# The tail of V with two halves side by side, and three reorderings, in a fused retention, expert-attention and mixing kernel

## The chip, the cores and the metric

The kernel runs on one core of a Trainium2 chip. The metric is the device time of one execution in microseconds; where several executions are timed, the median stands for them. All products are made in float32 by splitting each operand into a high part and a low part (xh and xl for x, WH and WL for the projection weights): a product is the sum of high times high, high times low and low times high, three matmuls into one PSUM accumulator.

## The reference

Eight batches, 576 positions, 8 retention heads of 64, then 4 experts with heads of 64, model width 512. Cut to what matters:

```python
# 1. retention: decayed causal linear attention
Dmat = np.where(rel >= 0, gamma[:, None, None] ** rel[None, :, :], 0.0)
x = ((q @ k.T / 8) * Dmat) @ v                 # per batch and head -> [B, S, 512]
# 2. top-2 of 4 experts, each a causal softmax attention with its own Q, K, V, Wo
logits = x @ w_gate                            # softmax over the top two -> w
a = softmax(causal(scale * (x @ wq[e]) @ (x @ wk[e]).T))
out += mask * w * (a @ (x @ wv[e]) @ wo[e])
# 3. mixing over positions and channels
theta = x @ w_theta
y = w_tok_r @ (x * cos(theta)) + w_tok_i @ (x * sin(theta))
u = x + y
return u + relu(u @ w_ch)
```

## The kernel before

The 576 positions are cut into five chunks, four of 128 rows and a tail of 64 (`ROWS`, lines 22 to 25). The kernel has three stages on the same core. In the first, retention of one batch and the attention of the batch before it run interleaved; the second makes theta and the cosines of the finished outputs; the third does the mixing. All the edits lie in the first stage.

**The loop of attention (lines 644 to 729).** A unit is one batch b, one pair p of experts and one chunk m of queries; there are 80 (`nu`), ten to a batch. At step t TensorE gets, in this order: the scores of unit t (`at_scores`, matmuls at L336), projections named by `more` in `SLOTS` (L45), the transposes of the probabilities of unit t-1 (`at_trans`, L383, with the copy PSUM to PT at L388), then what `between` names: "O" for outputs of a finished group of chunks (`at_out`, L402), or one of the visits R1 to R5. The groups of chunks are (0), (1, 2) and (3, 4). `ready` is the list of output groups finished by an earlier step, `outs` that of this one. The last batch has no next one to work for; its ten steps, and one more, follow `LAST` (L57) instead: projections, the product of theta's weights with Wo (`F0`, `F1`), and early tiles of the second stage (`T`); there all finished outputs run at the end of their own step.

**A visit (`ret_step`, L203).** It advances the retention of batch b+1 by one chunk c: `scale` (L124) has GpSimd multiply the chunk's values by the decay into vp; `ret_state` (L151, matmuls at L158) adds to the 64x64 states S; `ret_scores` (L135, matmuls at L143) makes the scores, masked into sm by VectorE (L147); `ret_values` (L164, matmuls at L173 and L180) makes the outputs px, which VectorE scales into xt (L190), ScalarE copies to xh (L192) and GpSimd subtracts into xl (L193); then `ret_values` issues the loads of a later chunk through `loads` (L113). These products are pairs of 64x64 blocks on two quadrants of TensorE, two generators side by side: the values as `off`, states and scores as `diag`. If the visit has outputs to do (`mid`), it runs all but the last four steps of the values, then the outputs, then one more state beside the last four steps. Of the visits of a batch, R1 and R2 have both outputs in their middle and such a state after; the visit R4 has outputs, but no state after. The first batch has no attention beside it: `ret_first` (L219) and lines 538 to 568 run its chunks one after the other at the start, where the decay product of a later chunk is issued behind the xl of the chunk at hand (L197).

**Projections.** `proj_v` (L262) makes V and the gate's logits of one chunk: its rows of x are the stationary operand, 4 blocks of 128 channels, 260 columns of weights moving (256 of V, 4 of the gate), three products: twelve matmuls for a chunk, the tail included, whose stationary operand has 64 columns. ScalarE copies PSUM to V and to the logits (L277, L278). `proj_qk` (L235, L246) makes U from Q and KN from K; KN goes through four DMA transfers on SP's queue into KK (L252), the layout that the scores read.

**The order of the work.** TensorE's order in the first stage is the order of the code (`manual_schedule`, L412). The other engines and SP's queue of DMA issues are put in order by a planner before the run, which places each instruction by its priority and its simulated readiness; `issue_after` in the code holds an instruction behind another in that order. SP issues one transfer after the other, each on the waits that it needs, so a transfer that waits holds those behind it. PSUM has eight buffers named w that all of the first stage share. The tiles of the retention live in the pool `ret`; it is released at step nu-11, and the pools for Wo, theta's weights and the outputs (w2, wol, wa) take its space. At that step `fuse_load` (L507) issues eight loads of 256 columns of Wo (`wost`) and four of theta's weights (`th`), and `load_o` (L573) loads the outputs (`ol`) and the gate's rows (`og`) of a finished batch, which GpSimd multiplies (L580). At step nu-10 `fuse_split` (L527) splits all eight `wost` tiles into high and low parts, on ScalarE (L106) and VectorE (L107). Meanwhile the float64 weights of the third stage are converted in small jobs (`convert`, L461), eight small instructions on VectorE, ScalarE and GpSimd each.

Of the kernel before, what the change touches and what calls it, by code (L numbers as in the profile page):

```python
# [10 lines left out]
F32 = mybir.dt.float32  # L11
# [12 lines left out]
NCH = 5  # L24
# [39 lines left out]
def tile_kernel(ctx: ExitStack, tc: tile.TileContext, qk, kv, w1, wo, wot, wd, cst, out):  # L64
# [43 lines left out]


    MARK = {}  # L110
    QKT, KVT, XT, VP, SM, RAW = {}, {}, {}, {}, {}, []

    def loads(b, c):  # L113
        R = ROWS[c]
# [46 lines left out]
        o = SB[(k + 1) % 4]  # L161
        MARK["S"] = nc.vector.tensor_add(o, pS, SB[k % 4]) if k else nc.scalar.activation(o, pS, AF.Copy)

    def ret_values(b, c, first=False):  # L164

        R = ROWS[c]
        t, vp = QKT[b, c], VP[b, c]
        px = ps1.tile([128, 4, R], F32, name="w", bufs=WB, padded_shape=[128, 4, 128])
        for j in range(R // 64):
            sm = SM.pop((b, 2 * c + j))  # L170
            for x in range(4):
                for s in range(2):
                    nc.tensor.matmul(px[half(1 - s), x, half(j)], vp[half(s), j, x, :], sm[half(s), x, :],  # L173
                                     start=j == 0 and x == 0, stop=False, skip_group_check=True)
                yield
        for j in range(R // 64):
            k = 2 * c + j
            for x in range(4 if k else 0):
                for s in range(2):
                    nc.tensor.matmul(px[half(1 - s), x, half(j)], SB[k % 4][half(s), x, :], t[half(s), x, half(j)],  # L180
                                     start=False, stop=False, skip_group_check=True)
                yield
        for x in (QKT, KVT, VP):
            x.pop((b, c))
        cs = slice(c * C, c * C + R)
        if c == 0:
            XT[b] = (w1p.tile([128, 4, S], F32R, name="xh", bufs=1),
                     w1p.tile([128, 4, S], F32R, name="xl", bufs=1))
        xt = ret.tile([128, 4, R], F32, name="xt", bufs=2, padded_shape=[128, 4, 128])
        MARK["xt"] = nc.vector.tensor_mul(xt, px, gt[:, :, cs])  # L190
        xh, xl = XT[b]
        MARK["xh"] = nc.scalar.activation(xh[:, :, cs], xt, AF.Copy)  # L192
        MARK["xl"] = nc.gpsimd.tensor_sub(xl[:, :, cs], xt, xh[:, :, cs])  # L193
        nx = (b, c + LDB) if c + LDB < NCH else (b + 1, c + LDB - NCH)
        if nx[0] < B:
            loads(*nx)
        if RAW and first and c:  # L197
            with tc.issue_after(MARK["xl"].ins):
                scale()

    BLOCKS = {0: ((0, (4,)),), 1: ((0, (5, 6)),), 2: ((0, (7, 8)),), 3: ((1, (0, 1)), (1, (2,))), 4: ((1, (3,)),)}

    def ret_step(b, c, mid=None):  # L203

        if RAW:
            scale()
        diag = [ret_state(b, 2 * c + 1)] if c < NCH - 1 else []
        diag += [ret_scores(b + x, ks) for x, ks in BLOCKS[c] if b + x < B]
        last = (b, c + 1) if c < NCH - 2 else (b + 1, 0) if c == NCH - 1 and b + 1 < B else None
        off = ret_values(b, c)  # L210
        n = (12, 16, 16, 16, 8)[c]
        for _ in zip_longest(chain(*diag), islice(off, n - 4) if last and (mid or c == NCH - 1) else off):
            pass
        if mid:
            mid()
        for _ in zip_longest(ret_state(last[0], 2 * last[1]) if last else (), off):
            pass

    def ret_first(b, c, nx, scores):  # L219

        diag, off = [], []
        if 0 <= c < NCH - 1:
            diag.append(ret_state(b, 2 * c + 1))
        diag += [ret_scores(nx[0], ks) for ks in scores]
        if nx and nx[1] < NCH - 1:
            diag.append(ret_state(nx[0], 2 * nx[1]))
        if c >= 0:
            off.append(ret_values(b, c, True))
        for _ in zip_longest(chain(*diag), chain(*off)):
            pass  # L230

# [30 lines left out]
    def proj_v(b, c):  # L262
# [6 lines left out]
        R = ROWS[c]  # L269
        cs = slice(c * C, c * C + R)  # L270
        ps = ps1.tile([128, NV], F32, name="w", bufs=WB, padded_shape=[128, 512])
        for x, W in ((xh, WH), (xh, WL), (xl, WH)):
            for kt in range(4):
                nc.tensor.matmul(ps[:R], x[:, kt, cs], W[:, kt, w0:w0 + NV], start=x is xh and W is WH and kt == 0,  # L274
                                 stop=x is xl and kt == 3)
# [248 lines left out]
            nc.sync.dma_start(th.bitcast(F32), TT[kt])  # L524
            FW[kt] = (th, FW[kt])

    def fuse_split():  # L527
        for a in FP:
            with tc.issue_after(MARK["act"].ins), tc.issue_after(MARK["dve"].ins):
                split(*a)  # L530

# [28 lines left out]
    for k in range(4):  # L560
        with tc.issue_after(MARK["xt"].ins), tc.issue_after(MARK["xh"].ins):
            split_w1(0, k)
    w1s.release()
    work(-1, "v1")
    ret_first(0, 3, (0, 4), [(8,)])
    work(-1, "v2 k00")
# [86 lines left out]
    for t in range(nu + 1):  # L653
# [27 lines left out]
        if b < B - 1:  # L681
            if between[:1] == "R":
                c = int(between[1])
                x = b + 1
                def mid():
                    for o in ready:
                        at_out(*o)
# [3 lines left out]
                outs = ready + outs  # L691
        else:
            work(b, between)
            for o in ready + outs:
                at_out(*o)
            outs = []
        work(b, after)


# [7 lines left out]
        if t == nu - 11:  # L707
            assert not jobs[0]
            ret.release()
            w2 = pool("w2")  # L710
            WOH, WOL, MH, ML = [w2.tile([128, 2, DM], F32R, name=x) for x in ("WOH", "WOL", "MH", "ML")]
            wol = pool("wol")
# [2 lines left out]
            load_o(0)  # L715
            load_o(1)
        if t == nu - 10:
            fuse_split()
        if t == nu - 7:
            w1p.release()  # L720
            wa.release()
# [262 lines left out]
```

## Time and profile before

| what | us |
| --- | --- |
| three timed runs | 881.51, 885.5, 885.87 |
| their median | 885.5 |
| the profiled execution | 882.19 |
| its span in the trace | 880.4 |
| TensorE's matmuls busy | 858.9 (98% of the span) |
| TensorE's weight loads busy (they overlap the matmuls) | 795.3 (90%) |
| VectorE busy | 622.2 (71%) |
| ScalarE busy | 456.2 (52%) |
| GpSimd busy | 219.0 (25%) |

The span begins with the first instruction recorded and ends with the last; what the profiled execution has beyond it lies before and after. The profiled execution is one more than the three timed ones. In the views, PE is TensorE's matmuls, PEld its weight loads, DVE is VectorE, ACT ScalarE, POOL GpSimd and SPq SyncE's DMA issues. A line names line, engine and operation, then the tile written and the tiles read, the shape (partitions by elements) and the count; in brackets the idle time of the engine before it and what ended that. "issue" as a releaser means that the trace shows nothing that the instruction waited for. A float32 matmul that is not split appears as two records.

### The profile page before, as it was taken

How to read it: one execution, taken by the hardware profiler on the slowest of the kernel's cores; microseconds unless marked ns; L12 is line 12 of the kernel's file. 1: busy time of each engine (PE TensorE's matmuls, PEld its weight loads, DVE VectorE, ACT ScalarE, POOL GpSimd, SP SyncE). 2: the span in 40 equal slices, each digit the busy share in tenths (PEclk: the TensorE clock that was granted, in tenths of full speed). 3: DMA queues.
4: the chain of work that ended last, by engine and by line, in shares of the span. 5: the costliest groups of instructions: out<-in, count | busy, mean ns of one | idle time of the engine just before them, and what ended most of it. 6: DMA issues, size and time to landing. Idle time of an engine off the chain costs nothing.

```text
span 880.4 us, 25571 instructions
## 1 busy us (share of the span) xinstructions
PE 858.9 (98%) x10072; PEld 795.3 (90%) x10072; DVE 622.2 (71%) x1729; ACT 456.2 (52%) x1258; POOL 219.0 (25%) x268
## 2 busy tenths in 40 slices
PE   7899999999999999998999999999999999999998
PEld 6888889888888989897879999999989999999998
DVE  4588787878788897876768777676377765766632
ACT  1366657666675766666676345353244533444320
POOL 2425163543525454341300112010110102001010
PEclk9999999999999999999999999999999999999999
DMA  9757677676867676548674343422526233151411
GB/s 316 243 151 242 165 222 192 192 239 186 242 174 225 203 212 183 155 117 238 189 257 164 76 115 49 120 36 53 150 54 141 55 99 94 31 128 25 97 37 54
DMA packets 140440, 130.30 MB, mean 148 GB/s; under 512 B 75808, under 2 KB 114976, under 8 KB 140320
## 3 DMA queue, kind: packets, MB, share of 16 engines
q1 hardware_dynamic: 140176, 128.39, 52.4%
q8 instruction: 79, 1.29, 0.6%
q0 software_dynamic: 144, 0.28, 0.2%
q14 instruction: 41, 0.34, 0.1%
HBM read 78.03 MB, written 32.00 MB: 125 GB/s over the span
## 4 chain that ended last, share of the span: by engine, by line
PE 85%; DMA 5%; DVE 5%; issue 2%; POOL 1%; ACT 1%; SPq 1%; DVEq 0%; ACTq 0%; POOLq 0%
PE acc L786 22%; PE w L246 10%; PE w L101 6%; PE w L102 6%; PE w L103 6%; PE w L336 6%; PE w L274 5%; PE w L402 5%; PE w L383 5%; PE w L786 3%; PE w L158 3%; PE w L143 2%; DMA kt<-qk 2%; DMA kv<-kv 2%; DMA raw<-wd 1%
## 5 line engine op out<-in xcount | busy, mean ns | idle before, releaser
L786 PE MATMUL acc<-TK,zh 128*128 128x288 f32 (+2 forms) x896 | 156.7, 296 | 0.5 <-ACT ob L406 0.5
L786 PEld LDWEIGHTS acc<-TK,zh 128*128 128x128 f32 x896 | 132.2, 189 | 1.2 <-issue 0.6
L344 ACT ACTIVATE P<-P,st 128x128 f32<-128x128 f32 (+4 forms) x160 | 95.4, 598 | 40.4 <-DVE st L339 40.1
L802 POOL TENSOR_TENSOR ul<-u,uh 128x576 fp32r<-128x576 f32 x16 | 24.2, 1535 | 312.6 <-ACT uh L801 312.6
L786 PE MATMUL acc<-TK,zl 128*128 128x288 f32 (+1 forms) x448 | 96.1, 296 | 0.0
L106 ACT ACTIVATE zh<-cs 128x512 fp32r<-128x512 f32 x64 | 40.3, 630 | 76.8 <-PE acc L786 61.7
L336 PE MATMUL w<-KK,U 128*64 128x288 f32 (+4 forms) x384 | 77.2, 328 | 0.8 <-issue 0.5
L339 DVE CUSTOM_DVE_ANT_0 P<-w,cm 128x128 f32<-128x128 f32 (+4 forms) x160 | 71.1, 477 | 7.0 <-PE w L336 6.1
L107 DVE TENSOR_TENSOR zl<-cs,zh 128x512 fp32r<-128x512 f32 x64 | 45.1, 705 | 43.5 <-ACT zh L106 42.8
L786 PEld LDWEIGHTS acc<-TK,zl 128*128 128x128 f32 x448 | 72.5, 189 | 0.0
L626 ACT ACTIVATE cs<-cs,quarter 128x256 f32<-128x256 f32 x72 | 36.5, 507 | 55.4 <-DVE cs L624 55.2
L629 DVE SCALAR_TENSOR_TENSOR cs<-cs,x 128x512 f32<-128x512 f32 x72 | 50.7, 706 | 18.3 <-ACT cs L627 17.6
L383 PE MATMUL w<-ident,P 128*128 128x128 f32 (+2 forms) x480 | 60.1, 260 | 1.4 <-DVE sm L147 1.3
L402 PE MATMUL w<-PT,V 128*64 128x192 f32 (+3 forms) x576 | 56.8, 325 | 4.3 <-DVE PT L388 3.0
L336 PEld LDWEIGHTS w<-KK,U 128*128 128x128 f32 (+1 forms) x384 | 54.0, 171 | 7.3 <-issue 1.6
L193 POOL TENSOR_TENSOR xl<-xt,xh 128x512 fp32r<-128x512 f32 (+1 forms) x40 | 47.9, 1197 | 51.1 <-ACT xh L192 51.1
L480 POOL TENSOR_TENSOR r<-r,ex 128x192 f32<-128x192 f32 (+1 forms) x51 | 29.5, 578 | 119.8 <-ACT hl L481 37.7
L192 ACT ACTIVATE xh<-xt 128x512 fp32r<-128x512 f32 (+1 forms) x40 | 23.6, 589 | 66.1 <-DVE xt L190 66.0
L103 PE MATMUL w<-uh,CH 128*128 128x288 f32 x192 | 56.6, 295 | 0.0
L102 PE MATMUL w<-ul,CH 128*128 128x288 f32 x192 | 56.5, 294 | 0.0
L101 PE MATMUL w<-uh,CH 128*128 128x288 f32 x192 | 56.5, 294 | 0.0
L402 PEld LDWEIGHTS w<-PT,V 128*64 128x64 f32 (+1 forms) x576 | 35.8, 135 | 22.0 <-issue 4.8
(153 smaller groups left out, 2347.4 us busy)
## 6 DMA issues: line engine op xcount, KB each, us to landing
KK<-KN SPq DMA_DIRECT2D x128, 144.0 KB
kt<-qk SPq DMA_DIRECT2D x32, 512.0 KB
kv<-kv SPq DMA_DIRECT2D x32, 512.0 KB
raw<-wd SPq DMA_DIRECT2D x43, 192.0 KB
xd<-xb SPq DMA_DIRECT2D x126, 64.0 KB
out<-u SPq DMA_DIRECT2D x28, 288.0 KB
u<-xd SPq DMA_DIRECT2D x28, 288.0 KB
td<-hl SPq DMA_DIRECT2D x27, 192.0 KB
```

What stands on the lines that cost most here:

```text
L101: nc.tensor.matmul(ps, ah, bh, start=first, stop=False)
L102: nc.tensor.matmul(ps, ah, bl, start=False, stop=False)
L103: nc.tensor.matmul(ps, al, bh, start=False, stop=last)
L193: MARK["xl"] = nc.gpsimd.tensor_sub(xl[:, :, cs], xt, xh[:, :, cs])
L246: nc.tensor.matmul(ps, W[:, kt, w0:w0 + 128], x[:, kt, sl], start=x is xh and W is WH and kt == 0, stop=x is xl and kt == 3)
L336: nc.tensor.matmul(ps[s][:R], U[:, s, rs], KK[:, s, x, j0:j1], start=x == 0, stop=x == 1)
L339: MARK["dve"] = nc.vector.tensor_tensor_reduce(Ps[s][:R, j0:j1], ps[s][:R], cm[:R, o + j0:o + j1], 1.0, st[:R, 0, s:s + 1] if i else 3.0e3 ...
L344: MARK["act"] = nc.scalar.activation(Ps[s][:R, :n], Ps[s][:R, :n], AF.Exp, bias=st[:R, last, s:s + 1], scale=-1.0, accum_out=SUM[p][:R, m, ...
L383: nc.tensor.transpose(tp[:w, j, :], Ps[s][:R, j * C:j * C + w], ident[:R, :R])
L402: nc.tensor.matmul(po[s * 64:s * 64 + 64, c0:], V[:ROWS[j], j, 2 * p + s, :], v, start=j == 0, stop=j == last, skip_group_check=True)
L629: nc.vector.scalar_tensor_tensor(z, cs, -1.0, x2[:, None, ds].to_broadcast([128, 2, 256]), op0=OP.mult, op1=OP.mult)
L786: nc.tensor.matmul(acc[d][j], A[:, dc], TK[:, kt, W, t0:t1], start=q == 0 and n == 0, stop=q == 8 and n == 2)
```

## The change

The tail of V: for the chunk of 64 rows, `ret_values` also makes a tile x2 with xh and xl of those rows side by side, 128 columns, by one more copy on ScalarE and one more subtraction on GpSimd. `proj_v` uses it as the stationary operand against WH and then WL, eight matmuls into 128 partitions of PSUM: the upper 64 hold xl's products. ScalarE copies those to a side tile, and two additions on VectorE make V and the logits. The product of xl and WL, left out elsewhere, is included here. The new pool `x2p` stands between w1s's release and the release at step nu-11.

The early reorder: `ret_first` issues `scale` at its head for c > 0, and `ret_values` no longer issues it at its end.

Visit ends: `ret_step` puts the further state behind the scores in the same `diag` stream, runs all of the values beside it, and the outputs after them.

The late reorders: in the last batch the outputs finished at a step run at the end of the next one, as `ready`, except at t = nu, where both run; and `fuse_split` splits the four tiles of the transposed Wo at step nu-10 and the four others two steps later.

```diff
--- before.py
+++ after.py
@@ -108,7 +108,7 @@
 
 
     MARK = {}
-    QKT, KVT, XT, VP, SM, RAW = {}, {}, {}, {}, {}, []
+    QKT, KVT, XT, XB, VP, SM, RAW = {}, {}, {}, {}, {}, {}, []
 
     def loads(b, c):
         R = ROWS[c]
@@ -161,7 +161,7 @@
         o = SB[(k + 1) % 4]
         MARK["S"] = nc.vector.tensor_add(o, pS, SB[k % 4]) if k else nc.scalar.activation(o, pS, AF.Copy)
 
-    def ret_values(b, c, first=False):
+    def ret_values(b, c):
 
         R = ROWS[c]
         t, vp = QKT[b, c], VP[b, c]
@@ -191,41 +191,43 @@
         xh, xl = XT[b]
         MARK["xh"] = nc.scalar.activation(xh[:, :, cs], xt, AF.Copy)
         MARK["xl"] = nc.gpsimd.tensor_sub(xl[:, :, cs], xt, xh[:, :, cs])
+        if R == 64:
+            x2 = x2p.tile([128, 4, 2, 64], F32R, name="x2t", bufs=1)
+            nc.scalar.activation(x2[:, :, 0, :], xt, AF.Copy)
+            nc.gpsimd.tensor_sub(x2[:, :, 1, :], xt, x2[:, :, 0, :])
+            XB[b] = x2.rearrange("p k a r -> p k (a r)")
         nx = (b, c + LDB) if c + LDB < NCH else (b + 1, c + LDB - NCH)
         if nx[0] < B:
             loads(*nx)
-        if RAW and first and c:
-            with tc.issue_after(MARK["xl"].ins):
-                scale()
 
     BLOCKS = {0: ((0, (4,)),), 1: ((0, (5, 6)),), 2: ((0, (7, 8)),), 3: ((1, (0, 1)), (1, (2,))), 4: ((1, (3,)),)}
 
-    def ret_step(b, c, mid=None):
+    def ret_step(b, c, outs=None):
 
         if RAW:
             scale()
         diag = [ret_state(b, 2 * c + 1)] if c < NCH - 1 else []
         diag += [ret_scores(b + x, ks) for x, ks in BLOCKS[c] if b + x < B]
         last = (b, c + 1) if c < NCH - 2 else (b + 1, 0) if c == NCH - 1 and b + 1 < B else None
-        off = ret_values(b, c)
-        n = (12, 16, 16, 16, 8)[c]
-        for _ in zip_longest(chain(*diag), islice(off, n - 4) if last and (mid or c == NCH - 1) else off):
+        if last:
+            diag.append(ret_state(last[0], 2 * last[1]))
+        for _ in zip_longest(chain(*diag), ret_values(b, c)):
             pass
-        if mid:
-            mid()
-        for _ in zip_longest(ret_state(last[0], 2 * last[1]) if last else (), off):
-            pass
+        if outs:
+            outs()
 
     def ret_first(b, c, nx, scores):
 
         diag, off = [], []
+        if c > 0:
+            scale()
         if 0 <= c < NCH - 1:
             diag.append(ret_state(b, 2 * c + 1))
         diag += [ret_scores(nx[0], ks) for ks in scores]
         if nx and nx[1] < NCH - 1:
             diag.append(ret_state(nx[0], 2 * nx[1]))
         if c >= 0:
-            off.append(ret_values(b, c, True))
+            off.append(ret_values(b, c))
         for _ in zip_longest(chain(*diag), chain(*off)):
             pass
 
@@ -269,6 +271,18 @@
         R = ROWS[c]
         cs = slice(c * C, c * C + R)
         ps = ps1.tile([128, NV], F32, name="w", bufs=WB, padded_shape=[128, 512])
+        if R == 64:
+            x2 = XB.pop(b)
+            for W in (WH, WL):
+                for kt in range(4):
+                    nc.tensor.matmul(ps, x2[:, kt, :], W[:, kt, w0:w0 + NV], start=W is WH and kt == 0,
+                                     stop=W is WL and kt == 3)
+            t = x2p.tile([64, NV], F32, name="vt", bufs=1)
+            nc.scalar.activation(t, ps[64:], AF.Copy)
+            tv, pv = [x[:, :E * D].rearrange("p (e d) -> p e d", e=E) for x in (t, ps[:64])]
+            nc.vector.tensor_add(V[:64, c, :, :], pv, tv)
+            nc.vector.tensor_add(l[:64, c, :], ps[:64, E * D:], t[:, E * D:])
+            return
         for x, W in ((xh, WH), (xh, WL), (xl, WH)):
             for kt in range(4):
                 nc.tensor.matmul(ps[:R], x[:, kt, cs], W[:, kt, w0:w0 + NV], start=x is xh and W is WH and kt == 0,
@@ -524,8 +538,9 @@
             nc.sync.dma_start(th.bitcast(F32), TT[kt])
             FW[kt] = (th, FW[kt])
 
-    def fuse_split():
-        for a in FP:
+    def fuse_split(n):
+        while FP[n:]:
+            a = FP.pop(0)
             with tc.issue_after(MARK["act"].ins), tc.issue_after(MARK["dve"].ins):
                 split(*a)
 
@@ -561,6 +576,7 @@
         with tc.issue_after(MARK["xt"].ins), tc.issue_after(MARK["xh"].ins):
             split_w1(0, k)
     w1s.release()
+    x2p = pool("x2p")
     work(-1, "v1")
     ret_first(0, 3, (0, 4), [(8,)])
     work(-1, "v2 k00")
@@ -691,9 +707,8 @@
                 outs = ready + outs
         else:
             work(b, between)
-            for o in ready + outs:
+            for o in ready if t < nu else ready + outs:
                 at_out(*o)
-            outs = []
         work(b, after)
 
 
@@ -707,6 +722,7 @@
         if t == nu - 11:
             assert not jobs[0]
             ret.release()
+            x2p.release()
             w2 = pool("w2")
             WOH, WOL, MH, ML = [w2.tile([128, 2, DM], F32R, name=x) for x in ("WOH", "WOL", "MH", "ML")]
             wol = pool("wol")
@@ -715,7 +731,9 @@
             load_o(0)
             load_o(1)
         if t == nu - 10:
-            fuse_split()
+            fuse_split(4)
+        if t == nu - 8:
+            fuse_split(0)
         if t == nu - 7:
             w1p.release()
             wa.release()
```

## Rows read from the trace of the kernel before

**Rows 1.** The page: busy time by engine; queues: packets, MB, share.

```profile
PE 858.9 (98%) x10072; PEld 795.3 (90%) x10072; DVE 622.2 (71%) x1729; ACT 456.2 (52%) x1258; POOL 219.0 (25%) x268
...
q8 instruction: 79, 1.29, 0.6%
```

**Rows 2.** Timeline at 289.9: start, us, engine, line, operation, [idle before].

```profile
291.73 0.74 POOL L193 TENSOR_TENSOR xl<-xt,xh 128x256 fp32r<-128x256 f32 x1
...
293.16 0.64 PE L274 MATMUL w<-WH,xh 128*64 128x260 f32 x4
...
294.12 0.64 PE L274 MATMUL w<-WH,xl 128*64 128x260 f32 x4
```

**Rows 3.** Chain that ended last, 278 to 281: start, us, what.

```profile
278.64 1.44 PE w L274 x12
```

**Rows 4.** Groups by line and form: count, busy us, mean ns, idle before.

```profile
L162 DVE TENSOR_TENSOR S<-w,S 128x256 f32<-128x256 f32 x56 | 23.3, 416 | 6.0 <-PE w L158 3.6 <-PE w L180 2.0
L190 DVE TENSOR_TENSOR xt<-w,gt 128x512 f32<-128x512 f32 x32 | 21.7, 679 | 1.4 <-PE w L180 1.4
L274 PEld LDWEIGHTS w<-WH,xh 128*128 128x128 f32 x128 | 18.1, 189 | 1.8 <-ACT xh L192 1.0 <-DVE U L260 0.4 <-ACT WH L106 0.2
L274 PEld LDWEIGHTS w<-WH,xh 128*64 128x64 f32 x32 | 4.1, 134 | 0.0
L192 ACT ACTIVATE xh<-xt 128x256 fp32r<-128x256 f32 x8 | 3.4, 419 | 8.5 <-DVE xt L190 8.5
```

**Rows 5.** TensorE by stretch: busy, granted clock, DMA share, GB/s.

```profile
265.41:266.97 1.56, 1.56 (x98) 1.00 0.00 0
268.20:268.82 0.62, 0.62 (x34) 1.00 0.56 116
271.64:273.67 2.03, 2.03 (x131) 1.00 0.57 180
```

**Rows 6.** Waits: engine, line, us in total, times, longest.

```profile
PEld w L383 <- DVE sm L147: 2.8, 5, 0.6
```

**Rows 7.** Timeline, 20.6 to 25.2, PEld, GpSimd and TensorE.

```profile
20.61 0.13 PEld L180 LDWEIGHTS w<-kt,S 64*64 64x64 f32 x1 [2.79 <-issue]
...
22.79 1.31 POOL L193 TENSOR_TENSOR xl<-xt,xh 128x512 fp32r<-128x512 f32 x1 [5.20 <-ACT xh L192]
...
25.14 0.27 PE L158 MATMUL w<-vp,kv 64*64 64x64 f32 x2 [2.69 <-POOL vp L128]
```

**Rows 8.** Stretches, all engines: busy (instructions), granted clock, DMA share, GB/s.

```profile
20.61:22.30 1.69, 1.69 (x107) 1.69 (x106) 1.29 (x3) 0.23 (x1) 0.00 (x0) 1.00 0.98 182
26.30:29.60 3.30, 3.30 (x58) 3.07 (x61) 2.08 (x3) 2.67 (x6) 1.96 (x2) 0.50 0.66 178
```

**Rows 9.** Queue of instructions, 18.1 to 19.3, then 22.2 to 23.7.

```profile
q8 instruction: 1, 0.02, 5.8%
...
q8 instruction: 1, 0.02, 5.6%
```

**Rows 10.** Timeline of the late stops, 392 to 443 (SPq: SP's issues).

```profile
392.51 0.74 POOL L193 TENSOR_TENSOR xl<-xt,xh 128x256 fp32r<-128x256 f32 x1
...
393.28 1.00 SPq L511 DMA_DIRECT2D wost<-wot  x2
...
407.55 0.42 DVE L107 TENSOR_TENSOR WOL<-wost,WOH 128x256 fp32r<-128x256 f32 x1 [1.28 <-ACT WOH L106]
...
410.22 0.44 PE L402 MATMUL w<-PT,V 128*64 128x128 f32 x4 [2.97 <-DVE PT L388]
...
424.24 1.31 SPq L252 DMA_DIRECT2D KK<-KN  x2
...
428.14 0.68 PE L336 MATMUL w<-KK,U 128*128 128x128 f32 x4
...
440.30 0.38 PE L383 MATMUL w<-ident,P 128*128 128x128 f32 x2
...
442.46 0.43 PE L402 MATMUL w<-PT,V 128*64 128x128 f32 x2 [1.01 <-ACT PT L388]
```

## The prediction, made before the changed kernel ran

> **What bounds the kernel now.** I read the page's engine shares first, then the groups by line and form, then the timeline wherever TensorE stands still. TensorE is busy for 98% of the span [rows 1]; V at 71% and the others lower can matter only where one of them is late for a particular matmul. So the question for each edit is whether it takes work off TensorE's own queue or ends one of its few stops, and, for a stop, what is late next. The profiled execution took 882.19 us (span 880.4, about 1.8 around it). It belongs with the low one of the three timed runs (881.51); the other two are 885.5 and 885.87. I make the sum against the profile and say at the end how I place it between these.
>
> **The tail of V.** Before, each of 8 batches issues 12 matmuls with 64 stationary columns, 260 moving ones. The rows show the first group of four at 293.16 and the third at 294.12 [rows 2]: 8 in 0.96 us, 0.12 each. With 128 stationary columns twelve take 1.44 us [rows 3], 0.12 each as well. So 8 matmuls replace 12 at the same price: 4 x 0.12 = 0.48 a batch, 3.84 over eight. Weight loads do grow, 134 to 189 ns [rows 4]; as 0.12 a matmul is kept with either, I take them as hidden. The Trainium skill, page "TensorE: Matmul & The Clock Gate", section "LDWEIGHTS (loading the stationary operand)", says that a load's time goes with its columns; where that were exposed, the eight loads of the new form would eat nearly all of the gain, while the rows say it is covered.
>
> What it adds: ScalarE copies x once more (0.42, as the xh copy of 256 columns [rows 4]), GpSimd subtracts once more (0.74 [rows 2]), ScalarE's copy of V becomes one to the side tile, and VectorE gets two adds (0.42 by the S add of 256 columns [rows 4], the gate's 4 columns less). None of these engines is the bound, and V's tail is read only in the next batch's outputs, so the adds are costed at nothing; without that cover they would be 0.6 a batch. But the first new matmul reads both halves of x2, so the stationary operand is complete only after GpSimd's second subtraction. In the batch shown xl starts at 291.73 [rows 2]; two subtractions end at 291.73 + 2 x 0.74 = 293.21, and TensorE is there at 293.16. That is a wait of about 0.1; the matmuls queued behind are at_out's and the transposes, which all wait with it. By the same reading of the other batches I charge it in three: 0.3. Its ends: 0, and the subtraction wholly bare, 0.74 x 8 = 5.9; the row puts it at the low end.
>
> **Visit ends.** Before, a visit with a finished group runs its retention matmuls, the outputs, and then 32 more retention records (16 fp32 matmuls recorded twice). The two bursts take 1.56 and 0.62, an unbroken 128 takes 2.03 [rows 5]: 0.15 less per visit. Only the visits R1 and R2 have outputs in the middle; R4's already stand at the end, R3 and R5 have none. 7 batches x 2 = 14 visits, 2.1 at most. After R1 the next transposes wait for VectorE's product sm in five cases, 2.8 us together [rows 6]. VectorE sets the time there and takes the 0.15 back. So 9 x 0.15 = 1.35. Bounds: 0 and 2.1, plus 2.8 if another PSUM buffer comes free first. No DMA is added; the loads that values() issues go out earlier by about the outputs' time (266.97 to 268.20 [rows 5]), which I count as nothing.
>
> **The early reorder.** scale() now runs at the head of ret_first, so vp of chunk 3 no longer queues on GpSimd behind xl of chunk 1 (22.79 to 24.10), which waits for TensorE's own results. Before, TensorE stops 2.69 us and goes on at 25.14, released by that vp [rows 7]. In the new order the product needs only its kv, and GpSimd does nothing from 20.61 to 22.30 [rows 8]. Yet I do not count 2.7. Ahead of this stop lies one at 20.61 of 2.79 us for which the trace shows no releaser ("issue") [rows 7]. In that time one packet of the instruction queue q8 moved, between 18.1 and 19.3, and TensorE went on 1.3 us after. The next q8 packet falls in 22.2 to 23.7 [rows 9]. There are 79 such packets for 10072 matmuls and as many weight loads [rows 1], 255 instructions a packet. From 20.61 to 22.30 TensorE used 107 + 106 = 213 [rows 8]. So 42 more, a third of a microsecond, and it needs the packet that lands at 23.7; with the same 1.3 after it TensorE goes on at 25.0. Before, it passed that point at 25.14 + 0.33 = 25.47. Gain 0.5, the stop merely changing its cause. Behind it the granted clock is 0.50, the 1.2 GHz level, from 26.30 to 29.60 [rows 8], after these two stops; 3.3 us do 1.65 of work there. With the stop nearly as long as before I leave this as it is. Ends: 0, and 2.8 + 1.65 = 4.5.
>
> **The late edits.** Before, TensorE stands 2.97 us until 410.22, as outputs need a PT copy that sits on VectorE behind the splits of wo and conversion work [rows 10]. Both edits remove that: the wo splits come two steps later, and outputs one step later, with 20 matmuls of the group before put in their place. What is late next: the second half of KK of the second head pair. SP issues two of its four transfers only at 424.24, behind the gate rows, and the scores that read them start at 428.14 [rows 10]; the second goes out half of the two's 1.31 later, near 424.9. This queue runs on landings and on GpSimd, not on TensorE, so a TensorE that comes 3 us earlier finds nothing. Bounds: nothing kept if the transfers land as they are read, 3.0 if they had landed long before. Issue to reader is 3.2 us for the second of the two, with the DMA engines in use; I take nothing kept. It can even cost: the first load of this queue leaves at 393.28 as xl of the last batch ends (392.51 + 0.74) [rows 10]. That load goes into the retention pool's space, and the new subtraction reads the same xt 0.74 longer, so the queue starts 0.7 late; I charge 0.6. For the same reason the 0.48 of the last batch's tail is lost. Past that point the wait at 440.30 to 442.46 remains: 2.16 us in which TensorE did two transposes and two outputs, some 0.35 of work, waiting for ScalarE's PT copy [rows 10]. In the new order 20 older outputs stand there, so 1.8 go. Late sum: -1.8 + 0.6 = -1.2, ends +0.6 and -4.8.
>
> **Instruction supply elsewhere.** A retention burst of 128 passes about one packet's worth of instructions in 2.03 us [rows 5], and the new order makes R2 such a burst too. Where a packet's end falls on it, a short stop like the one at 20.61 is possible. I charge 0.5, ends 0 and 2.
>
> **Sum.** Tail 7 x 0.48 - 0.3 = 3.1; visits 1.35; early 0.5; late 1.2; supply -0.5. Together 5.6 us less: 876.6 by the profiled execution. The four executions known average 883.8 and the median of three is 885.5; 5.6 off the average is 878.2, which I forecast.
>
> **Rivals.**
> 1. The supply doesn't hold TensorE early. The Trainium skill, page "Runtime: NRT & Kernel Launch", section "Instruction fetch mechanics", calls the crossing of a 16 KiB block "mostly hidden"; by that rule the whole early stop goes. The stop at 20.61 speaks against it here. As a mechanism of this kernel: the packet is asked for sooner, the 2.8 goes, and the stretch at 1.2 GHz with it, 4.5 in place of 0.5: 878.2 - 4.0 = 874.2. Chance 0.18.
> 2. The late gain is kept: SP's order is laid anew, and the KK transfers stand ahead of the second set of gate rows. Then 3.0 is kept, with the last tail's 0.48: 878.2 - 4.1 = 874.1. For it: two of the four already stand ahead. Against: nothing in the diff moves them. Chance 0.12.
> 3. The tail doesn't do what it says: the 128-column loads, 189 against 134 ns, are bare, 8 x 0.055 = 0.44 of the 0.48. The sum falls by 3.1: 881.3. The equal 0.12 speaks against it. Chance 0.12.
> 4. Slower: after R1 and R2 the transposes get another PSUM buffer, the one that xt frees. VectorE then does S (0.42) and xt (0.68 [rows 4]) after sm, 1.1 a visit, 14 visits, 15.4. Less the 5.6: 893.6. It is slower than no change from 0.4 a visit, and by more than 0.5% from 0.72. For it: five such waits already stand there, on sm. Against: sm's place among the allocations hardly moves. Chance 0.06.
> The forecast itself has 0.52, with a range of its own of 875.5 to 881.5.
>
> **Chances.** A measurement of this kernel tells about 0.5% from no change, 4.4 us: faster means below 881.1. Rivals 1 and 2 lie there, 0.30, and about seven tenths of the forecast, 0.36. Rival 3 and the rest are "same", 0.28. Slower is rival 4, 0.06. Range 872.5 to 884.0: it holds the forecast, rivals 1 to 3 with their scatter, and leaves out rival 4 and both early and late gains at their far ends.
>
> **What would show it.** Right: eight L274 matmuls of 128 columns and 0.12 for each tail; one retention burst of 128 at R1 and R2; vp of chunk 3 on GpSimd ahead of 22; TensorE still stopped to about 25, now with no releaser; scores of the last batch's second pair waiting for KK near 428; no wait at 440. Wrong: new waits of L274 for x2 beyond 0.1, the transposes after R1 or R2 waiting longer than 0.6, or a clock at full level from 26 on, which is rival 1.

## The result, and the profile after

The changed kernel takes 889.08 us (median of 20, 883.6 to 895.07) against 883.34 (median of 20, 879.08 to 887.09): 1.0067 of the time before, 95% interval 1.0053 to 1.0081. It is slower by about 6 us where 5 less had been forecast. Its profiled execution is the longest of the twenty (895.07, span 892.9), so a loss read from this trace is larger than the median's; compared with the profiled execution of before (882.19) it is 12.9.

The page after, engines and queue q8, answering to [rows 1]:

```profile
PE 861.2 (96%) x10040; PEld 795.4 (89%) x10040; DVE 625.1 (70%) x1745; ACT 458.5 (51%) x1258; POOL 224.5 (25%) x276
...
q8 instruction: 79, 1.29, 0.6%
```

TensorE has 32 matmuls less and is busy for 2.3 us more, at 96% of a longer span. To find where, I took from the timeline the start of each step's first score matmul and compared step by step. The table sums each step of the loop over the seven batches that have visits, minus the same sum before (us, one profiled execution each; the last column is all of the last batch):

| kernel | 3 (R1) | 4 (R2) | 5 (R3) | 6 | 7 (R4) | 8 (R5) | 9 (tail) | last batch |
| --- | --- | --- | --- | --- | --- | --- | --- | --- |
| changed | -1.1 | +1.5 | +16.6 | +3.3 | -2.0 | -1.2 | -3.1 | 0.0 |
| visits only | -1.1 | +1.2 | +8.6 | +2.3 | -0.8 | -1.2 | -0.5 | 0.0 |
| old visits | 0.0 | 0.0 | +9.0 | -0.3 | -1.8 | -1.2 | -3.2 | -1.6 |
| tail only | 0.0 | 0.0 | +9.4 | -0.2 | -1.7 | -0.9 | -3.2 | +1.4 |
| changed, pad 64 | -1.1 | -0.2 | +3.6 | +2.3 | -1.9 | -1.2 | -3.2 | -2.0 |
| old visits, pad 64 | 0.0 | 0.0 | 0.0 | 0.0 | +1.9 | -1.2 | -3.3 | -2.1 |
| before, pad 88 | 0.0 | 0.0 | +11.8 | +1.2 | -1.9 | -1.2 | -0.4 | -0.9 |
| before, pad 56 | 0.0 | 0.0 | 0.0 | 0.0 | +0.5 | -1.2 | -0.6 | -1.7 |
| pad 64, ob first | -1.1 | -0.2 | +1.3 | +4.2 | -1.9 | -1.2 | -2.8 | -2.4 |
| pad 64, ob and V first | -1.1 | -0.2 | +1.2 | -0.2 | 0.0 | -1.2 | -3.2 | -3.0 |

Nearly everything that is lost is lost at R3 and just after it (steps 5 and 6), a visit whose instructions the change does not touch; the 1.5 at R2 goes with the shift of the blocks, too (-0.2 with pad 64). Step 5 of batches 0, 4 and 5 as stretches, TensorE alone (busy, count, granted clock, DMA share, GB/s), first before, then changed, then the changed kernel with 128 more records of matmuls and weight loads ahead ("pad 64", below):

```profile
63.09:67.95 4.86, 4.86 (x161) 1.00 0.79 263
268.83:273.67 4.84, 4.84 (x160) 1.00 0.84 263
319.62:324.49 4.87, 4.87 (x160) 1.00 0.91 264
```

```profile
62.13:69.16 7.03, 5.52 (x157) 1.00 0.63 200
270.50:279.00 8.50, 5.34 (x157) 0.96 0.79 256
325.96:334.83 8.87, 5.51 (x157) 0.90 0.84 255
```

```profile
62.05:67.77 5.72, 5.39 (x157) 1.00 0.75 229
266.28:271.13 4.85, 4.85 (x157) 1.00 0.78 264
317.19:322.04 4.85, 4.85 (x157) 1.00 0.76 256
```

In the changed kernel TensorE stands for 1.5 to 3.4 us in each of the three, and each of the seven batches has one such stop at R3, the shortest 0.7 us. The waits of its matmuls between 58 and 400 for which no releaser is shown (us in total, times, longest):

```profile
PE w L180 <- issue: 5.8, 3, 3.4
...
PE w L158 <- issue: 5.0, 3, 3.2
...
PE w L143 <- issue: 1.2, 1, 1.2
```

These are the burst's own instructions; before, no such row exists for L143, L158 or L180. One of them, with the share of the instruction queue between 275.7 and 276.9:

```profile
278.23 0.27 PE L158 MATMUL w<-vp,kv 64*64 64x64 f32 x2 [3.16 <-issue]
```

```profile
q8 instruction: 1, 0.02, 5.1%
```

TensorE stands for 3.16 us while a packet of q8 runs, and goes on about 1.4 us after its end, as at 20.61 before [rows 7, 9]. That the packets bring the instructions in blocks of equal size shows in the counts between one such stop and the next, in the changed kernel and in the run "before, pad 88", which has none of the edits (matmuls and weight loads counted in brackets, then VectorE, ScalarE, GpSimd):

```profile
68.30:120.73 52.43, 50.70 (x883) 45.20 (x883) 43.07 (x148) 33.55 (x109) 21.85 (x32) 1.00 0.69 198
120.73:172.41 51.68, 50.46 (x882) 45.16 (x882) 41.55 (x144) 33.96 (x111) 23.15 (x33) 1.00 0.73 201
```

```profile
70.36:123.72 53.36, 50.88 (x882) 45.66 (x881) 43.02 (x146) 33.64 (x111) 22.12 (x33) 1.00 0.69 200
123.72:176.65 52.93, 52.01 (x882) 46.95 (x883) 40.67 (x140) 33.52 (x109) 21.18 (x30) 0.97 0.67 190
```

883 + 883, 882 + 882, 882 + 881, 882 + 883: within two of 1764, seven times 252. Seven packets of the queue pass between two stops in either kernel. And one batch of each kernel (from its first score to the next batch's):

```profile
143.23:194.42 51.19, 50.55 (x884) 45.67 (x881) 43.12 (x146) 33.95 (x112) 24.66 (x34) 1.00 0.72 211
```

```profile
143.96:195.94 51.98, 50.76 (x880) 45.22 (x877) 42.88 (x147) 34.25 (x111) 25.36 (x35) 1.00 0.73 207
```

884 + 881 = 1765 before, 880 + 877 = 1757 after. A batch is almost exactly seven packets, so where a block ends in R3's burst in one batch, one ends there, a few records on, in the next. In the kernel before one ends there as well (counted under "Visits only"), but its packet comes soon enough for TensorE not to stop.

The stops over 3 us at R3 in batches 4 and 5 are followed by stretches at the 1.2 GHz level (granted clock 0.53 and 0.50), which is what step 6 pays (1.2 and 2.2 us):

```profile
278.20:281.40 3.20, 3.17 (x35) 0.53 0.85 245
334.00:338.00 4.00, 4.00 (x33) 0.50 0.95 284
```

The tail and R2's burst did what they were to do. The tail by form (count, busy us, mean ns, idle before), answering to [rows 3, 4]:

```profile
L278 PE MATMUL w<-WH,x2t 128*128 128x260 f32 x32 | 5.5, 295 | 0.0
...
L278 PEld LDWEIGHTS w<-WH,x2t 128*128 128x128 f32 x32 | 4.4, 188 | 0.6 <-POOL x2t L197 0.2
...
L197 POOL TENSOR_TENSOR x2t<-xt,x2t 128x256 fp32r<-128x256 f32 x8 | 6.0, 745 | 0.0
```

Waits for x2 come to 0.2 us over all batches, and the one unbroken burst of R2 in batch 4 takes what [rows 5] gave for R3's 131:

```profile
267.36:269.38 2.02, 2.02 (x130) 1.00 0.07 18
```

The early stop only changes its cause: vp of chunk 3 now runs at 18.39, and TensorE still stands until 24.74, with no releaser [rows 7].

```profile
18.39 1.03 POOL L128 TENSOR_TENSOR vp<-kv,gam 128x512 f32<-128x512 f32 x1 [0.97 <-DMA kv<-kv]
```

```profile
24.74 0.27 PE L180 MATMUL w<-kt,S 64*64 64x64 f32 x2 [2.13 <-issue]
```

In the last batch the waits of [rows 10] are gone and others stand in their place, the loads of theta's weights and KK:

```profile
426.93 0.50 PE L101 MATMUL w<-th,wt 128*128 128x512 f32 x1 [0.97 <-DMA th<-tt]
...
428.79 0.50 PE L101 MATMUL w<-th,wt 128*128 128x512 f32 x1 [0.89 <-DMA th<-tt]
...
443.48 0.41 PE L350 MATMUL w<-KK,U 128*128 128x128 f32 x2 [0.94 <-DMA KK<-KN]
```

### The profile page after: what moved, and what is told of

Its sections match the earlier page's. It is cut to its first block, busy times and chain, and to the rows that moved or that the text cites. A ratio compares the mean times of both kernels' runs of the same rounds, so it can differ in the third digit from the quotient of the medians.

```text
span 892.9 us, 25549 instructions
## 1 busy us (share of the span) xinstructions
PE 861.2 (96%) x10040; PEld 795.4 (89%) x10040; DVE 625.1 (70%) x1745; ACT 458.5 (51%) x1258; POOL 224.5 (25%) x276
## 4 chain that ended last, share of the span: by engine, by line
PE 83%; DVE 5%; DMA 3%; issue 3%; ACT 2%; SPq 1%; POOL 1%; ACTq 0%; DVEq 0%; POOLq 0%
PE acc L804 22%; PE w L248 9%; PE w L101 6%; PE w L102 6%; PE w L103 6%; PE w L350 5%; PE w L416 5%; PE w L288 5%; PE w L397 4%; PE w L804 3%; PE w L143 3%; PE w L158 2%; DMA KK<-KN 2%; PE w L180 1%; PE acc L101 1%
## 5 line engine op out<-in xcount | busy, mean ns | idle before, releaser
L397 PEld LDWEIGHTS w<-ident,P 128*128 128x128 f32 (+2 forms) x480 | 47.0, 138 | 8.7 <-DVE sm L147 3.3
```

The source lines that it names most:

```text
L397: nc.tensor.transpose(tp[:w, j, :], Ps[s][:R, j * C:j * C + w], ident[:R, :R])
```

## The experiments

Theory PLACE: what counts is at which matmul a block of instructions ends against the bursts. Theory ORDER (later LOADS): the unbroken R2 sends kt and kv out ahead of the packet that R3 needs. Later a third, BUFFER, for what the new visits cost by themselves. All ratios are to the kernel before on the same chip, with 95% intervals.

**Visits only.** The kernel before with the new `ret_step`:

```diff
-        for _ in zip_longest(chain(*diag), islice(off, n - 4) if last and (mid or c == NCH - 1) else off):
...
+        if last:
+            diag.append(ret_state(last[0], 2 * last[1]))
+        for _ in zip_longest(chain(*diag), ret_values(b, c)):
```

> The kernel before with the new order of the visits alone (no middle; values whole, outputs after them). The traces of before (883.3) and after (889.1) differ first at the retention visit R3: between the starts of steps 5 and 6 the changed kernel loses 1.4 to 4.0 us in each of six batches, in stops for which no releaser is shown, each 1.2 to 1.6 us after a packet of the instruction queue has ended. Theory ORDER: the unbroken burst of R2 sends its loads of kt and kv out before the outputs, and the instruction packet that R3 needs queues behind them; then this edit alone costs what the changed kernel loses at R3: 890 to 894, stops of 1 us or more at R3. Theory PLACE: what matters is at which matmul a block of 256 instructions ends, which the count of instructions ahead sets; this edit leaves the count as before, so 881 to 884 and no stop over 0.7 at R3. Rival CLOCK: the loss is only the 1.2 GHz stretches; then 883 with no change of stops.

888.73, ratio 1.0071 (1.0049 to 1.0094). The stops are there, though the count is that of before:

```profile
PE w L180 <- issue: 4.2, 5, 2.2
...
PE w L143 <- issue: 1.0, 1, 1.0
```

The time lies in neither theory's range, nearer to ORDER's. But the order also moves the 24 records of R2's outputs behind the burst's last 64, so that other instructions stand where the block that ends in R3 begins, and this run alone does not tell the two apart. It does show that the end of a block is not all that counts, so PLACE stands from here on for where a block begins and where it ends. The same number of records lies ahead of R3 as before, so by the count a block ends at the same one. Up to its stop at R3 in batch 3, which begins at 223.43, this run has passed 112 matmuls and 110 weight loads of step 5; the kernel before passes the same place at 220.80 and does not stop (this run, then before):

```profile
218.98:223.43 4.45, 4.45 (x112) 4.05 (x110) 4.31 (x15) 1.96 (x8) 3.02 (x4) 1.00 0.40 122
```

```profile
216.77:220.80 4.03, 4.03 (x113) 3.81 (x110) 3.93 (x17) 1.73 (x6) 2.15 (x4) 1.00 0.55 161
```

What differs is the packet: before, it runs from 216.96 to 218.39, just after step 5 has begun; here from 221.88 to 223.14, 2.9 us after.

**Old visits.** The changed kernel with `ret_step` of before (the same diff reversed).

> The changed kernel with the visits in their old order (outputs in the middle). ORDER: the stops at R3 go, the tail's gain and the early gain stay: 877 to 880. PLACE: the count of instructions is that of the changed kernel, the ends of blocks fall near R3 as there: 886 to 890. Mixed: 880 to 886.

883.21, ratio 1.0021 (1.0002 to 1.0040): between the two. The stops at R3 did not go with the visits:

```profile
PE w L158 <- issue: 3.8, 3, 1.3
...
PE w L180 <- issue: 2.8, 2, 1.5
```

**Tail only.** The kernel before with x2, `x2p` and the new branch of `proj_v`.

> The kernel before with the tail of V alone (8 matmuls in place of 12 in each batch). ORDER: the visits are those of before, no stops at R3, the tail's 0.3 to 0.5 a batch comes through: 879.5 to 881.5. PLACE: eight records fewer per batch move the ends of blocks by 8 to 56 along the stream; 881 to 888, with stops at a visit that before did not have.

886.33, ratio 1.0047 (1.0028 to 1.0067): the tail alone makes the kernel slower, although step 9 gains the full 3.2. What it loses is at R3, with eight records a batch that are no longer there:

```profile
PE w L180 <- issue: 4.7, 3, 1.9
...
PE w L158 <- issue: 3.0, 2, 1.6
```

ORDER falls here, since its visits are the old ones. The last batch costs 1.4 more.

**Changed, pad 64.** All edits kept; only the warm-up differs, so that every block ends 128 records earlier:

```diff
-    warm_up(WARM)
+    pw = ps1.tile([128, 128], F32, name="w", bufs=WB, padded_shape=[128, 512])
+    for _ in range(WARM + 64):
+        nc.tensor.matmul(pw[:64, :64], warm[:, :64], warm[:, :64], start=True, stop=True)
```

> The changed kernel with 114 short warm-up matmuls (64 columns) in place of 50 of 128, in the time in which TensorE waits for the first load: 128 more records of matmuls and weight loads ahead, so each block of 256 ends 128 records earlier in the work, nothing else altered. PLACE: from the changed kernel's own trace, with a constant 3.3 us from one block's start to the next one's use, the stops sum to 4.5 as it is and to 0 with this shift: 880 to 884, the stops at R3 gone. ORDER: the packet still waits 3.5 to 5.3 us behind kt and kv: 887 to 891, stops merely at other matmuls.

878.71, ratio 0.9955 (0.9937 to 0.9972): 1.1% less than the changed kernel by instructions that compute nothing. The three stretches of step 5 above show it; no wait of a matmul without a releaser is left in a burst between 58 and 400. VectorE, ScalarE, GpSimd and SP's queue work through the same instructions in the same order as without the pad (so, too, in the two runs of the kernel before with a pad), so that behind the warm-up only the place of the blocks differs. PLACE, and even past its range.

**Hold the loads.** The loads that R2 issues, one visit later in the code:

```diff
+    HELD = []
...
-            loads(*nx)
+            HELD.append(nx)
+        while HELD and (c != 1 or not b):
+            loads(*HELD.pop(0))
```

> The changed kernel; the kt and kv loads that R2 issues (a chunk needed 25 us later) go out with those of R3 instead, one visit later; TensorE's instructions and their number are unchanged. Theory LOADS (the packet of instructions that R3 needs queues behind R2's kt and kv on the DMA engines, 3.5 to 5.3 us against 0.3 to 1 elsewhere): the packet comes at once, the stops at R3 go, 878 to 882. Theory PLACE alone (where blocks end against the bursts, at a constant time per packet): nothing moves, 887 to 891.

886.9, ratio 1.0060 (1.0039 to 1.0081). It tells nothing of LOADS: the planner put the transfers at the same places of SP's queue, so this is the changed kernel once more, and shows how well its ratio repeats.

**Old visits, pad 64.**

> The changed kernel with the visits in their old order and the same 128 records ahead as in the run of 878.7. By the trace of the run with the old visits (883.2) the stops at R3 sum to 9; shifted by 128, at 4 us a packet, to 0.1. PLACE with a cost of the new visit order by itself (scores of R3 waiting for a PSUM buffer that ScalarE's output copy frees, about 0.7 a batch, and 0.5 after it): 873 to 876. Rival, the new order is neutral or a gain: 879 to 880.

876.04, ratio 0.9921 (0.9904 to 0.9937). As PLACE with a cost of the new visits had it (the top of its range): 3 us below the changed kernel with the same pad. One stop in a burst is left:

```profile
PE w L180 <- issue: 0.7, 1, 0.7
```

**Before, pad 88.** The warm-up as above, with 88 in place of 64, on the kernel before.

> The kernel before, nothing changed but 176 more records of warm-up matmuls ahead (138 short ones for 50). PLACE: by its own trace, at 3.3 us a packet, the stops go from 1.0 to 7.8, the worst place of sixteen: 887 to 893, as slow as the changed kernel with none of its edits. Rival (the old order does not mind where blocks end): 881 to 884.

891.44, ratio 1.0100 (1.0083 to 1.0116). With none of the edits the kernel before is slower than the changed one, by the same stops at the same visit:

```profile
PE w L180 <- issue: 5.4, 4, 1.7
...
PE w L158 <- issue: 3.1, 2, 2.2
```

This is the plainest proof of PLACE. Its packets at R3 begin 0.9 to 2.3 us after TensorE has begun the block before, but TensorE is through with that block, most of which is R3's burst, in 2.1 to 2.5 us. Its longest stop is followed by the lower clock:

```profile
123.72:126.00 2.28, 2.28 (x19) 0.71 1.00 235
```

**Old visits, loads held.**

> The changed kernel with the visits in their old order and R2's loads held for one visit. LOADS: the 9 us of stops at R3 go without any shift of the blocks: 874 to 877. PLACE alone: as without the hold, 882 to 884.

884.82, ratio 1.0028 (1.0012 to 1.0044). As with the other hold, SP's order is unchanged: a second take of the old visits.

**Loads held by a real wait.** As the first hold, and the held transfers wait for VectorE's read of R3's products:

```diff
...
+        for z in (x, y) if behind else ():
+            tc.add_manual_dep(z.ins, MARK["xt"].ins.name, mybir.DependencyInfo(
+                mybir.DependencyClass.Sync, mybir.DependencyReason.DATA), reason="behind R3")
...
```

> The changed kernel; the hold of the run before, now bound: the kt and kv loads that R2 and R3 issue may not start before VectorE has read R3's products (xt), so that after R2 only the half-size kt and no kv goes out. TensorE's instructions and their order are unchanged. LOADS: the packet that R3 needs is on its way within 1 us of being asked for, the stops at R3 go: 878 to 882. PLACE alone: packets take as long as before, 886 to 890. Something else on the queues holds the packet: no change of its 3.5 to 5.3 us although the loads are gone.

888.43, ratio 1.0059 (1.0036 to 1.0082). Now the loads do move; in batch 0 one kt of half size goes out after R2 and no kv:

```profile
60.41 0.56 SPq L118 DMA_DIRECT2D kt<-qk  x1
...
63.86 3.18 SPq L378 DMA_DIRECT2D gd<-nwt  x4
```

The stops in R3's burst shrink but do not go, and new ones come elsewhere (L162 and L184 are the burst's lines here, L254 is the projection of Q in step 8):

```profile
PE w L254 <- issue: 1.7, 3, 0.7
PE w L184 <- issue: 1.5, 3, 0.7
...
PE w L162 <- issue: 1.2, 2, 0.9
```

In this trace, then, R2's loads look like a part of why the packet is late, but its execution (885.35) is among the faster of its run and that of the changed kernel the slowest, and the medians show no time given back. At its stops in R3 of batches 1 to 3 the packet still begins 3.4 to 3.9 us after TensorE has begun the block before, against 3.5 to 5.3 in the changed kernel's first six. What holds it is open.

**Before, pad 56.**

> The kernel before with 112 more warm-up records ahead, the best place of sixteen by its own trace (stops 1.0 to 0 at 3.3 us a packet, 7.1 to 0 at 4): 879.5 to 882. It tells what of the 876.0 of the old visits with pad is the place of the blocks, and what the edits. Rival (the whole 7 us of that run is place): 876.

879.25, ratio 0.9961 (0.9946 to 0.9976). Half of the 7 us of "old visits, pad 64" is place. The same program, before, runs at 0.9961 or 1.0100 by its warm-up alone.

**Tail, pad 64.** The kernel with the tail alone and the pad.

> The kernel before with the tail of V alone, and 128 records ahead. Against the kernel before at its good place: 7 x 0.45 less by the tail itself, 1.3 more late (SP's queue of late loads starts 0.7 later, as in the run with the tail alone): 1.5 to 2 less than that run, 878 to 880. Rival, the tail's stationary operand or its additions cost something once the stops are gone: no gain against it.

878.45, ratio 0.9950 (0.9933 to 0.9968), against 0.9961 for before at its good place: 0.1% in the direction expected, and the intervals overlap, so the tail's net gain is not shown by these times. At step 9 the traces that have the tail show 2.8 to 3.9 us less, those without it 0.4 to 0.6.

**Pad 64, ob first.** The new visits lose 5.9 us at steps 5 and 6 with all blocks well placed. ScalarE and TensorE in the run "changed, pad 64" at R3 of batch 0:

```profile
65.26 0.63 ACT L192 ACTIVATE xh<-xt 128x512 fp32r<-128x512 f32 x1 [2.45 <-DVE xt L190]
65.80 0.35 ACT L420 COPY ob<-w 128x256 f32<-128x256 f32 x1
```

```profile
66.20 0.27 PE L143 MATMUL w<-kt 64*64 64x64 f32 x2 [0.24 <-ACT ob L420]
```

R2's output matmuls end at 62.1; ob, their copy out of PSUM, starts at 65.80, since the planner has xh ahead of it, which waits 2.45 us for VectorE. R3's scores wait for the buffer. The edit issues the outputs from within `ret_values`, ahead of xt and in the same order for TensorE, and holds xh behind ob in the planner's order:

```diff
...
+            if "ob" in MARK:
+                es.enter_context(tc.issue_after(MARK["ob"].ins))
             MARK["xh"] = nc.scalar.activation(xh[:, :, cs], xt, AF.Copy)
...
```

> The changed kernel with 128 records ahead (878.7), and on ScalarE, in seven places, the copy of R2's outputs (ob) put ahead of the copy of xh that the order had ahead of it; nothing else differs. In the run of 878.7 that copy starts at 65.80, 3.7 us after its matmuls end, because xh ahead of it waits for VectorE; R3's scores wait for the PSUM buffer that it frees, and steps 5 and 6 take 5.9 us more over seven batches than before. Theory BUFFER (the new visit order costs this by the late copy): 3.6 to 5.9 of that go, 873 to 875.5. Rival (the order of the visits costs by itself, or VectorE sets it): 878 to 880.

879.09, ratio 0.9959 (0.9943 to 0.9975): no change, the rival's number. But the wait did go, and came back one step later. In batch 2 V's copies start at 170.37, behind two conversion operations, and the next scores wait for them:

```profile
170.37 0.35 ACT L295 COPY V<-w 128x256 f32<-128x256 f32 x1
170.62 0.18 ACT L296 ACTIVATE lg<-w 128x4 f32<-128x4 f32 x1
```

```profile
170.85 0.30 PEld L354 LDWEIGHTS w<-KK,U 128*128 128x128 f32 x2 [0.80 <-ACT lg L296]
```

**R1 alone, pad 64.** Old visits but for R1.

```diff
...
+        if last and not c:
+            diag.append(ret_state(last[0], 2 * last[1]))
+            last = None
...
```

> Old visits and 128 records ahead (876.0), with the new order of the visit for R1 alone. From the steps of all runs with the new visits, step 3 takes 0.16 less in each of seven batches and nothing is given back at step 4: 874.5 to 875.5 (1.1 less). Rival (R1's gain is given back later, or R1's order is part of the 5.9 lost at R3): 876 to 878.

875.8, ratio 0.9934 (0.9916 to 0.9952), between the two ranges and against 0.9921 for the old visits: the 1.1 us at step 3 is in its trace, and the times do not show it. The trace says why: step 4 takes 0.9 more than before, 0.09 to 0.16 in each batch, so most of R1's gain is given back at once, as the rival had it.

**Pad 64, ob and V first.** As "ob first", and the conversions at step 5 held behind V's copies:

```diff
...
+        lg = nc.scalar.activation(l[:R, c, :], ps[:R, E * D:], AF.Copy)
+        if c == 0 and b:
+            MARK["act"] = lg
```

> The run with ob first (879.1), where the wait of R3's scores was gone (step 5 from 3.6 to 1.3 over seven batches) and came back one step later as scores waiting 0.8 for ScalarE's copies of V and the logits, which stand behind two conversion operations that wait for VectorE (step 6 from 2.3 to 4.2). Here those two stand behind V's copies as well. BUFFER (two late copies in a row, each holding a PSUM buffer): 3 to 5 us go, 874 to 876. Rival (the new visits make VectorE's work late, and whatever is next waits for it): the time moves again to another wait, 878 to 880.

875.44, ratio 0.9917 (0.9899 to 0.9934): 3.6 us less than with ob alone, step 6 from +4.2 to -0.2. BUFFER, in the second of two waits in series. Not all of it comes back: step 5 keeps 1.2, and step 7 takes 1.9 more than with ob alone. This, "old visits, pad 64" (0.9921) and "R1 alone, pad 64" (0.9934) have the lowest ratios; they can't be told apart. The first two lie clear of "before, pad 56" (0.9961), so there the edits gain beyond the place of the blocks.

## Why the prediction was wrong

- **The bound and the tail: right.** Step 9 gained the 3.1 summed over seven batches, though 0.4 to 0.6 of it stands in the three traces without the tail too, so that the tail's own is nearer 2.6; waits for x2 were 0.2 against 0.3 charged.
- **Visit ends: the gain right, a cost missed.** Steps 3 and 4 gained 1.1 and, where nothing stops, 0.2 (1.35 summed); by "R1 alone" step 4 gives back most of R1's gain, and R2's hides that. The transposes' wait for sm is 3.3 us in 5 cases, where it was 2.8 [rows 6]:

```profile
PEld w L397 <- DVE sm L147: 3.3, 5, 0.7
```

  Missed: the outputs moved behind the values, so their copy, which frees a PSUM buffer, fell behind xh on ScalarE. Steps 5 and 6 lose 5.9 us over seven batches with pad 64, and 1.0 once both copies are moved ahead. Rival 4 had the kind of it, a buffer that comes free late, but at the transposes, where nothing happened; it is at R3's scores and at the scores after them.
- **Early: right in kind.** The stop stayed and changed its cause; the first scores come 1.2 us earlier in this trace (0.5 forecast). In the ten profiled runs with the early order that point lies between 41.64 and 45.03, so its size is not settled.
- **Late: not settled.** 1.2 forecast; 0.0 in this trace, and from 2.5 more to 3.0 less in the nine other profiled runs with these edits, while the kernel before with pad 56 also shows 1.7 less. What is late next is KK, as said (0.94), and before it th, which was not said (2.1 in three waits).
- **Instruction supply elsewhere: the step that failed.** It was charged at 0.5, ends 0 and 2. It measures 1.1% of the time, some 10 us: 1.0067 with the blocks as they fell against 0.9955 with the same kernel shifted by 128 records. I had seen that a burst of 128 uses up a packet, and took a collision for a matter of chance that happens once or twice. It is not: a batch is seven packets long to within a few instructions, so it comes back in most batches (four to seven of the seven in the kernels that stop) or in none, and the eight records that the tail takes out are enough to move from the one to the other. Nor did I ask when a packet begins: at R3 it is up to 5.6 us after TensorE has begun the block before, and R2's earlier loads, which were counted as nothing, look like a part of that. The stop also costs more than its own length, as the slow stretches behind the long ones show. The Trainium skill, page "Runtime: NRT & Kernel Launch", section "Instruction fetch mechanics", gives a block as 16 KiB and 256 instructions, to which the 252 recorded ones come close; that its crossing is "mostly hidden" does not hold in this kernel, where it is worth 0.9961 or 1.0100 of the time by its place.
- **What is left of the sum.** With its blocks well placed the changed kernel (0.9955) and the kernel before (0.9961) can't be told apart: the gains that came true and the buffers' 5.9 us about cancel. That 878.71 with the pad lies next to the 878.2 forecast is chance.
- **Rivals.** 1: no, the early stop and the clock stayed. 2: no, KK is still late. 3: no, most of the tail's gain is there.

## What to carry to other kernels

Where TensorE is the bound and its instructions come in blocks, adding or removing matmuls moves the ends of all later blocks: time a change at two or three shifts of the blocks (some short matmuls in an idle moment at the start) before believing its sign. A stop with no releaser inside a dense burst, 1.2 to 1.6 us after a packet of the instruction queue has ended, is its mark here, and equal counts of instructions from one such stop to the next confirm it. When work that fills a PSUM buffer is moved later on TensorE, look where the copy that frees the buffer then stands on the copying engine, and at the next such copy too.

## What the runs showed of the hardware

The place of the blocks alone moved one and the same program from 0.9961 to 1.0100 of its time. A block is about 252 recorded matmuls and weight loads here (1763 to 1766 in seven). A packet runs for 0.9 to 1.6 us in the changed kernel. Counted 252 records back from a block's end in R3, it begins 0.6 us (batch 3 of the kernel before) to 5.6 us (batch 5 of "visits only") after TensorE has begun that block, and at the stops TensorE goes on 1.2 to 1.6 us after the packet's end; it stops where it is through with the block sooner. The stops of 3.2 and 3.4 us in the changed kernel were followed by 3 to 4 us at the 1.2 GHz level, and the one of 2.2 us at 123.72 in "before, pad 88" by granted clocks of 0.71 and 0.50; those of 1.1 to 1.3 us in the changed kernel were not.
